# Moving the first use of one weight load later, splitting the last sums, and issuing small transfers from another engine in an attention-plus-MLP gradient kernel

## The chip, the core and the metric

The kernel runs on one core of one Trainium2 chip. The metric is the device time of that core in microseconds (us). Before the change the median of three runs was 423.68 us (423.5 to 424.09).

Engines are named as the profile names them: PE (TensorE: matrix products), PEld (its weight loads), DVE (VectorE), ACT (ScalarE), POOL (GpSimd), SP (SyncE, which here only requests loads). In the traces "SPq" or "ACTq" is the engine's own issuing of a transfer.

## The reference

The forward function is a gate between one decode step of cached attention (32 heads, 4096 keys, head size 128) and a small MLP. The kernel computes its output and all gradients. Cut to what matters:

```python
q = (x @ wq)                                    # 640 -> 32 heads x 128
p = softmax(q . k_cache * Dh**-0.5)             # k_cache, v_cache: 32 x 4096 x 128, bf16
a = (p . v_cache) @ wo
h = x_B @ w1 + b1 ; b = (h * tanh(softplus(h))) @ w2     # w2: 1728 x 640
out = g * a + (1 - g) * b ,  g = sigmoid(sum(x * gate_w))
# returned: out and the gradients of x, k_cache, v_cache, wq, wo, w1, b1, w2, gate_w
```

K and V have to be read once and dK and dV, just as large, have to be written once. Each of the 32 heads has 1 MB of each of the four.

## The kernel before

K and V come in through four buffers each, requested by SP three heads ahead. PE and ACT transpose them, PE forms scores and sums, DVE forms dK and dV as outer products in two halves each, and POOL requests their stores. The MLP runs in the gaps. It is cut into steps that a host-side list hands out, at three "slots" in each head:

```python
def slot(h, p=2, d=1):
    # called three times per head: runs ready steps, at most p of kind "P" (PE)
    # and d of kind "D" (DVE); a step is ready if all steps it names ran in an EARLIER slot
    ...
def load_w2(c):                                  # w2 comes in three pieces, two buffers
    w2cs[c] = mlp.tile([FP, FCC, D], BF16, name="w2c", tag="w2c", bufs=2)
    nc.sync.dma_start(w2cs[c][:], w2_v[:, c * FCC:(c + 1) * FCC, :])
...  # (cut)
for c in range(NCH):                             # NCH = 3 pieces
    add(f"b{c}", "P", b_part(c), ("act2",) + ((f"badd{c - 1}", f"dw2_{c - 1}") if c else ()), H0)
    add(f"badd{c}", "T", b_add, (f"b{c}",), H0)
    for i in range(FCC):
        add(f"dh{c}_{i}", "D", dh_part(c, i), ("act2", f"w2_{c}"), H0)     # DVE reads w2c
    ...  # dw2a, dw2: DVE writes dw2 over w2c, then POOL stores it
    if c < 2: done[f"w2_{c}"] = -1               # the first two pieces are loaded at the start
    else:
        for k in range(4):                       # wait four slots for the buffer's store
            add(f"w2w{k}_{c}", "T", lambda: None, (f"w2w{k - 1}_{c}" if k else f"dw2_{c - 2}",), H0)
        add(f"w2_{c}", "T", lambda c=c: load_w2(c), (f"w2w3_{c}",), H0)    # REQUEST of piece 3
```

The step `w2_2` is done when the load has been *requested*, not when it has landed. The next slot, about 4 us later, may already put the first product with the third piece into DVE's program. DVE runs its program in order, so it waits there.

The start and the end of the kernel also matter here:

```python
nc.sync.dma_start(vec_rows[0:RC, :], x_rows)               # three loads of 1.3 KB, then
nc.sync.dma_start(vec_rows[RC:2 * RC, :], dy_rows)         # the big loads, all on SP
nc.sync.dma_start(vec_rows[2 * RC:3 * RC, :], gw_rows)
load_wq(0); load_wo(0); load_k(0); load_v(0); ...          # (cut)
...
dk_half(H - 1, 0); dk_half(H - 1, 1)
last = [st for st in steps if st[0].startswith("dx")]      # five DVE sums of 1024 columns
...  # the other steps; then the last weight gradient, whose store is the last big one:
nc.gpsimd.dma_start(dwq_v[:, :, CL:], dwq_l[:])
steps.extend(last)                                         # the five sums, 1.22 us each
...  # some 14 small DVE, PE and ACT steps on 128x5 values, then three stores of five rows:
nc.sync.dma_start(out0_rows, fin_rows[0:RC, :])
nc.sync.dma_start(out1_rows, fin_rows[RC:2 * RC, :])
nc.sync.dma_start(out9_rows, fin_rows[2 * RC:3 * RC, :])
```

## Time and profile before

| | before |
|---|---|
| time, median (range) | 423.68 us (423.5 to 424.09) |
| span of the profiled run | 423.3 us |
| moved by DMA | 165.06 MB |
| rate on the plateau | about 422 GB/s |
| 165.06 MB at 422 GB/s | 391.1 us |
| DVE, PE busy | 307.4 us (73%), 306.7 us (72%) |

The page of the kernel before: busy time by engine, then the span in 40 slices of 10.6 us, with busy tenths (9 is 90% or more) and the rate that the DMA engines moved.

```profile
PE 306.7 (72%) x6932; PEld 283.4 (67%) x6932; DVE 307.4 (73%) x794; ACT 174.5 (41%) x394; POOL 50.9 (12%) x92
...
DVE  3359466675699999758306999899999976637981
...
DMA  7999999999999999999983799999999999999991
GB/s 243 424 411 395 422 423 417 424 420 426 422 423 422 423 415 423 422 423 422 414 312 147 292 343 392 412 421 423 420 424 422 424 422 420 424 407 399 411 409 59
DMA packets 26336, 165.06 MB, mean 390 GB/s; under 512 B 2812, under 2 KB 2812, under 8 KB 10012
```

No compute engine is full, and the DMA engines are full nearly everywhere. The rate stands at about 422 GB/s, and three places fall below it: the start (slice 1), a hole (slices 21 to 25) and the end (slice 40). The Trainium skill, "DMA: Bandwidth & Descriptors", section Specifications, gives a fabric ceiling of 435 GB/s; the trace's plateau agrees with it within 3%.

It helps to turn the row of rates into a budget. A slice at rate r loses (422 − r)/422 of its 10.58 us. Summed over all slices that is 32.2 us, and 391.1 + 32.2 is the span of 423.3 us. By part: slices 1 to 4 lose 5.4 us, 21 to 27 lose 15.9 us, and 36 to 40 lose 10.7 us.

The waits of the same kernel: which engine and line waited for what, us in total, times, longest.

```profile
ACT tT L531 <- PE tr L529: 173.1, 138, 21.0
POOL out_dram L568 <- DVE dK_sb L551: 73.6, 10, 23.2
DVE junk L449 <- DMA w2c<-in_B_w_dram: 20.3, 1, 20.3
...
PE qc_ps L258 <- DMA wq_g<-in_A_wq_dram: 3.7, 2, 2.8
...
SPq L781 <- DMA out_dram<-dwq_l: 1.8, 1, 1.8
```

The chain that ended last, in order of time (start, duration, what), around the hole:

```profile
194.50 0.03 SPq L138
...
194.57 30.21 DMA w2c<-in_B_w_dram
...
224.81 0.04 DVE junk L449
```

And the windows of the hole and of the end: stretch in us, its length, busy us of each engine (instructions), granted clock, share of the 16 DMA engines, GB/s.

```profile
200.00:212.00 12.00, 4.80 (x113) 4.34 (x111) 4.52 (x12) 3.38 (x7) 1.06 (x2) 0.83 1.01 411
212.00:224.00 12.00, 0.00 (x0) 0.00 (x0) 0.00 (x0) 0.00 (x0) 0.00 (x0) 0.50 0.82 291
224.00:236.00 12.00, 10.15 (x183) 9.66 (x184) 9.63 (x25) 3.84 (x8) 1.07 (x2) 0.53 0.30 126
...
415.00:419.00 4.00, 0.28 (x1) 0.09 (x1) 0.38 (x2) 0.26 (x1) 0.00 (x0) 0.50 0.06 25
```

The load of the third piece is requested at 194.57 us and lands 30.2 us later, behind the loads already queued. DVE stands still for 20.3 us, and everything behind it in its program stands too: from 212 to 224 us no engine runs a single instruction. While they stand, the queued transfers finish, no new buffer comes free, and DMA falls to 126 GB/s.

The line for 415 to 419 us is worth remembering. A DMA share of 0.06 is one sixteenth, and 25 GB/s is about one sixteenth of 422. For those 4 us one single DMA engine was moving data and the other fifteen had finished.

The start, in the timeline (start, duration, engine, line, what):

```profile
0.74 0.36 SPq L108 DMA_DIRECT2D vec_rows<-in_A_x_dram  x1
...
1.81 0.41 SPq L127 DMA_DIRECT2D wq_g<-in_A_wq_dram  x1
```

The first big load is the fourth that SP issues, 1.07 us after the first.

### The profile page before, as it was taken

To read this page: it belongs to the slowest core of one execution; us is meant where nothing else is said; L and a number is where in the kernel's file an instruction comes from. 1 tells how busy PE (TensorE), PEld (TensorE's weight loads), DVE (VectorE), ACT (ScalarE), POOL (GpSimd) and SP (SyncE) were. 2 spreads that over 40 slices of the span, in tenths; PEclk is the share of its full clock that TensorE was granted. 3 is DMA by queue.
4 is the path that set the end of the run, shared out by engine and by line. 5 is a ranking of instruction groups with operands and counts; after the bars stand their busy time and mean duration, and the time that the engine had idled before them with its cause. 6 is when DMAs were issued, how large, how long until landed. Compare 5 with 4: busy or idle time off the path is not lost.

```text
span 423.3 us, 15629 instructions
## 1 busy us (share of the span) xinstructions
PE 306.7 (72%) x6932; PEld 283.4 (67%) x6932; DVE 307.4 (73%) x794; ACT 174.5 (41%) x394; POOL 50.9 (12%) x92
## 2 busy tenths in 40 slices
PE   2588799988989888488306978887787888838500
PEld 2587798888879777388306877787677787737400
DVE  3359466675699999758306999899999976637981
ACT  2265244444454545144201454645454455515200
POOL 0001111011001111111100111211111121103320
PEclk9999899999998999798855899999999899979855
DMA  7999999999999999999983799999999999999991
GB/s 243 424 411 395 422 423 417 424 420 426 422 423 422 423 415 423 422 423 422 414 312 147 292 343 392 412 421 423 420 424 422 424 422 420 424 407 399 411 409 59
DMA packets 26336, 165.06 MB, mean 390 GB/s; under 512 B 2812, under 2 KB 2812, under 8 KB 10012
## 3 DMA queue, kind: packets, MB, share of 16 engines
q1 hardware_dynamic: 14156, 82.03, 47.6%
q0 software_dynamic: 12112, 82.03, 46.9%
q8 instruction: 54, 0.88, 0.8%
q14 instruction: 14, 0.11, 0.1%
HBM read 82.03 MB, written 82.03 MB: 388 GB/s over the span
## 4 chain that ended last, share of the span: by engine, by line
DVE 32%; DMA 31%; PE 24%; ACT 7%; issue 3%; SPq 1%; ACTq 0%; DVEq 0%
DMA Kn<-in_A_k_cache_dram 13%; PE tr L529 8%; DVE dK_sb L551 8%; DMA w2c<-in_B_w_dram 7%; DVE dV_sb L551 7%; DMA out_dram<-dK_sb 7%; ACT tT L531 6%; DVE junk L354 4%; DMA Vn<-in_A_v_cache_dram 4%; PE sB L648 3%; PE h_ps L383 3%; PE sA L537 3%; PE sA L595 3%; DVE junk L484 2%; DVE junk L268 2%
## 5 line engine op out<-in xcount | busy, mean ns | idle before, releaser
L531 ACT COPY tT<-tr 128x512 f32<-128x512 f32 x256 | 143.1, 588 | 173.4 <-PE tr L529 173.1
L537 PEld LDWEIGHTS <-tT 128*128 128x128 bf16 x2048 | 76.6, 98 | 37.7 <-ACT tT L531 31.6
L529 PE MATMUL tr<-ident_bf,Kn 128*128 128x128 bf16 x1024 | 80.5, 232 | 6.2 <-DMA Kn<-in_A_k_cache_dram 5.1
L551 DVE TENSOR_TENSOR dV_sb<-p_bf,qd 128x2048 bf16<-128x2048 bf16 x64 | 78.0, 1218 | 8.4 <-DMA out_dram<-dK_sb 8.4
L551 DVE TENSOR_TENSOR dK_sb<-ds_bf,qd 128x2048 bf16<-128x2048 bf16 x64 | 77.7, 1215 | 0.0
L529 PE MATMUL tr<-ident_bf,Vn 128*128 128x128 bf16 x1024 | 74.0, 222 | 0.0
L529 PEld LDWEIGHTS <-Kn 128*128 128x128 bf16 x1024 | 67.7, 105 | 7.2 <-DMA Kn<-in_A_k_cache_dram 5.4
L537 PE MATMUL sA<-qdc,tT 128*128 128x48 bf16 x1024 | 49.1, 187 | 23.2 <-ACT dq_all L653 16.4
L529 PEld LDWEIGHTS <-Vn 128*128 128x128 bf16 x1024 | 64.2, 101 | 0.6
L537 PE MATMUL sB<-qdc,tT 128*128 128x48 bf16 x1024 | 46.7, 184 | 0.6 <-ACT tT L531 0.6
L568 POOL DMA_DIRECT2D out_dram<-dK_sb x31 | 19.0, 613 | 169.3 <-DVE rz L617 86.5
L648 PE MATMUL sB<-ds_bf,Kn 128*128 128x48 bf16 x1024 | 32.1, 185 | 9.7 <-DVE ds_bf L637 8.3
L578 POOL DMA_DIRECT2D out_dram<-dV_sb x32 | 18.4, 576 | 164.7 <-DVE dV_sb L551 75.1
L595 PEld LDWEIGHTS <-Vn 128*128 128x128 bf16 x1024 | 30.8, 96 | 10.7 <-issue 10.4
L595 PE MATMUL sA<-e_bf,Vn 128*128 128x48 bf16 x1024 | 31.5, 184 | 7.7 <-DVE zs L615 5.9
L648 PEld LDWEIGHTS <-Kn 128*128 128x128 bf16 x1024 | 29.3, 97 | 10.1 <-issue 10.1
L449 DVE SCALAR_TENSOR_TENSOR junk<-w2c,dm,db_bc 96x640 bf16<-96x640 bf16 x18 | 15.7, 874 | 20.5 <-DMA w2c<-in_B_w_dram 20.3
L599 DVE TENSOR_REDUCE m<-sA 128x1 f32<-128x32 f32 x32 | 6.0, 188 | 32.9 <-PE sA L537 32.7
L268 DVE SCALAR_TENSOR_TENSOR junk<-wo_g,da_bc 128x640 bf16<-128x640 bf16 x32 | 26.2, 820 | 4.3 <-DMA wo_g<-in_A_wo_dram 3.7
L603 PE MATMUL sA<-ident_f,m 128*128 128x128 f32 x32 | 9.6, 301 | 24.8 <-DVE m L599 24.8
L354 DVE SCALAR_TENSOR_TENSOR junk<-wq_g,dq_bc 128x1024 bf16<-128x1024 bf16 x20 | 24.4, 1218 | 0.2
L603 PEld LDWEIGHTS sA<-ident_f,m 128*128 128x128 f32 x32 | 4.5, 140 | 26.4 <-DVE m L599 26.2
(137 smaller groups left out, 293.5 us busy)
## 6 DMA issues: line engine op xcount, KB each, us to landing
Kn<-in_A_k_cache_dram SPq DMA_DIRECT2D x32, 1024.0 KB, 20.4
Vn<-in_A_v_cache_dram SPq DMA_DIRECT2D x32, 1024.0 KB, 27.1
out_dram<-dV_sb POOLq DMA_DIRECT2D x32, 1024.0 KB, 11.1
out_dram<-dK_sb POOLq DMA_DIRECT2D x31, 1024.0 KB, 11.8
wq_g<-in_A_wq_dram SPq DMA_DIRECT2D x4, 1280.0 KB, 20.5
wo_g<-in_A_wo_dram SPq DMA_DIRECT2D x8, 640.0 KB, 17.9
out_dram<-wo_g POOLq DMA_DIRECT2D x8, 640.0 KB, 11.6
out_dram<-dwq_t POOLq DMA_DIRECT2D x5, 896.0 KB, 11.9
```

Of the source, the lines that this page charges most:

```text
L268: nc.vector.scalar_tensor_tensor(junk[:, 0:D], in0=wos[g][:, i, :], scalar=1.0, in1=da_bc[:], op0=ALU.mult, op1=ALU.mult, accum_out=gp["do ...
L354: nc.vector.scalar_tensor_tensor(junk[:], in0=wqs[w][:, rc, :], scalar=1.0, in1=dq_bc[:, w * WG * Dh:(w + 1) * WG * Dh], op0=ALU.mult, op1 ...
L449: nc.vector.scalar_tensor_tensor(junk[0:FP, 0:D], in0=w2cs[c][:, i, :], scalar=m["dm"][:, fc:fc + 1], in1=db_bc[0:FP, :], op0=ALU.mult, op ...
L529: nc.tensor.transpose(tp[:, t, :], src[:, c * 8 + t, :], ident_bf[:])
L531: nc.scalar.copy(f32v(sb[:].rearrange("p a b -> p (a b)")), f32v(tp[:].rearrange("p a b -> p (a b)")))
L537: nc.tensor.matmul(out[:, j:j + W], lhsT=tb[:, t, :], rhs=vec.to_broadcast([P, W]), start=True, stop=True)
L551: nc.vector.tensor_tensor(dst[:, a:b, :].rearrange("p j (a b) -> p j a b", b=2), col[:, a:b, :].unsqueeze(2).to_broadcast([P, n, Dh // 2, 2]),
L568: nc.gpsimd.dma_start(dKv[h], st["dK"][:])
L578: nc.gpsimd.dma_start(dVv[h], st["dV"][:])
L595: nc.tensor.matmul(O, lhsT=vts[h][:, j, :], rhs=st["e"][:, j:j + 1].to_broadcast([P, W]), start=(j == 0), stop=(j == J - 1))
L603: nc.tensor.transpose(MM, m32[:].to_broadcast([P, P]), ident_f[:])
L648: nc.tensor.matmul(DQ, lhsT=kts[h][:, j, :], rhs=ds[:, j, 0:1].to_broadcast([P, W]), start=(j == 0), stop=(j == J - 1))
```

## The change

The change has three parts. The first separates the request of the third `w2` piece from its first use by eight more slots, so that the load lands before DVE gets there. The second halves the last dx sums by head group, so that only half of them remain for the end, and starts the gate's gradient earlier. The third takes the three small vector loads off SP's queue. The result is the same numbers from the same data.

```diff
-    nc.sync.dma_start(vec_rows[0:RC, :], x_rows)          # and the other two
+    nc.scalar.dma_start(vec_rows[0:RC, :], x_rows)
...
-        def dx(rc):
+        def dx(rc, c0, c1, slot_i):                       # sums columns c0:c1 only
...
-        if g % 2 == 1:
-            for rc in range(RC):
-                add(n(f"dx{rc}_"), "D", dx(rc), (n("dqb"),))
+        for rc in range(RC):
+            if g >= NG - 2:                               # last two groups: one half each
+                add(n(f"dx{rc}_"), "D", dx(rc, (g % 2) * GD, (g % 2 + 1) * GD, g - NG + 2 + NW - 1), (n("dqb"),))
+            elif g % 2 == 1:
+                add(n(f"dx{rc}_"), "D", dx(rc, 0, WG * Dh, g // 2), (n("dqb"),))
...
-            add(f"b{c}", "P", b_part(c), ("act2",) + ((f"badd{c - 1}", f"dw2_{c - 1}") if c else ()), H0)
+            add(f"b{c}", "P", b_part(c), ("act2", f"w2_{c}") + ((f"badd{c - 1}",) if c else ()), H0)
...
-                add(f"w2_{c}", "T", lambda c=c: load_w2(c), (f"w2w3_{c}",), H0)
+                add(f"w2l_{c}", "T", lambda c=c: load_w2(c), (f"w2w3_{c}",), H0)
+                for k in range(8):
+                    last = k == 7
+                    add(f"w2_{c}" if last else f"w2x{k}_{c}", "T", lambda: None,
+                        (f"w2x{k - 1}_{c}" if k else f"w2l_{c}",), H0)
...  # dgp, dg_ps, gg moved ahead of the last dx sums (cut)
-    nc.sync.dma_start(out1_rows, fin_rows[RC:2 * RC, :])
+    nc.scalar.dma_start(out1_rows, fin_rows[RC:2 * RC, :])
```

More of the change, by code (lines that the diff above doesn't have):

```diff
@@ L107 @@
     vec_rows = const.tile([3 * RC, P], BF16, name="vec_rows")
-    nc.sync.dma_start(vec_rows[0:RC, :], x_rows)
-    nc.sync.dma_start(vec_rows[RC:2 * RC, :], dy_rows)
-    nc.sync.dma_start(vec_rows[2 * RC:3 * RC, :], gw_rows)
+    nc.scalar.dma_start(vec_rows[0:RC, :], x_rows)
+    nc.scalar.dma_start(vec_rows[RC:2 * RC, :], dy_rows)
+    nc.scalar.dma_start(vec_rows[2 * RC:3 * RC, :], gw_rows)
     kts, vts, wqs, wos = {}, {}, {}, {}
@@ L220 @@
     NW = H // WG
-    dxp = const.tile([P, RC, NW + 2], F32, name="dxp")
+    dxp = const.tile([P, RC, NW + 3], F32, name="dxp")
     dq_bc = const.tile([P, H * Dh], BF16, name="dq_bc")
@@ L349, in dqb @@
             nc.scalar.copy(f32v(dq_bc[:, g * GD:(g + 1) * GD]), f32v(b_ps[:].rearrange("p a b -> p (a b)")))
-        def dx(rc):
+        def dx(rc, c0, c1, slot_i):
             def f():
                 w = g // 2
-                nc.vector.scalar_tensor_tensor(junk[:], in0=wqs[w][:, rc, :], scalar=1.0,
-                                               in1=dq_bc[:, w * WG * Dh:(w + 1) * WG * Dh],
-                                               op0=ALU.mult, op1=ALU.mult, accum_out=dxp[:, rc, w:w + 1])
+                nc.vector.scalar_tensor_tensor(junk[:, c0:c1], in0=wqs[w][:, rc, c0:c1], scalar=1.0,
+                                               in1=dq_bc[:, w * WG * Dh + c0:w * WG * Dh + c1],
+                                               op0=ALU.mult, op1=ALU.mult, accum_out=dxp[:, rc, slot_i:slot_i + 1])
             return f
@@ L485, in f @@
                                                in1=m["dh_bc"][:, a:b], op0=ALU.mult, op1=ALU.mult,
-                                               accum_out=dxp[:, rc, NW + k:NW + k + 1])
+                                               accum_out=dxp[:, rc, NW + 1 + k:NW + 2 + k])
             return f
@@ L717 @@
     nc.gpsimd.dma_start(dwq_v[:, :, CL:], dwq_l[:])
-    steps.extend(last)
-    while steps:
-        slot(H, 9, 9)
     assert len(dwqt) == RC
@@ L725 @@
     fin = C("fin", [P, 3 * RC])
-    ga = C("ga", [P, RC])
-    nc.vector.tensor_scalar(ga[:], a_acc[:], g_all[:], None, ALU.mult)
-    nc.vector.scalar_tensor_tensor(fin[:, 0:RC], in0=b_acc[:], scalar=omg_all[:], in1=ga[:], op0=ALU.mult, op1=ALU.add)
     amb = C("amb", [P, RC])
@@ L736 @@
     nc.tensor.transpose(dg_ps[:], dgp[:].to_broadcast([P, P]), ident_f[:])
+    ga = C("ga", [P, RC])
+    nc.vector.tensor_scalar(ga[:], a_acc[:], g_all[:], None, ALU.mult)
+    nc.vector.scalar_tensor_tensor(fin[:, 0:RC], in0=b_acc[:], scalar=omg_all[:], in1=ga[:], op0=ALU.mult, op1=ALU.add)
+    gg = C("gg", [P, 1])
+    nc.vector.tensor_tensor(gg[:], g_all[:], omg_all[:], ALU.mult)
+    for st in last[:2]:
+        st[2]()
     dg = C("dg", [P, 1])
     nc.vector.reduce_sum(dg[:], dg_ps[:], axis=AX.X)
-    gg = C("gg", [P, 1])
-    nc.vector.tensor_tensor(gg[:], g_all[:], omg_all[:], ALU.mult)
     dz = C("dz", [P, 1])
@@ L743 @@
     nc.vector.tensor_scalar(fin[:, 2 * RC:3 * RC], x_f, dz[:], None, ALU.mult)
+    for st in last[2:]:
+        st[2]()
     dxs = C("dxs", [P, RC])
```

## The prediction

The prediction counts the slices from 0, so its slices 20 to 26 are slices 21 to 27 in the rest of this document.

> **What bounds the kernel now.** The DMA engines. The page gives 165.06 MB; the windows 60-100, 100-140 and 300-340 us run at 422, 422, 423 GB/s. 165.06 MB at 422 is 391 us of the 423.3 us span. The Trainium skill, "DMA: Bandwidth & Descriptors", section Specifications, gives a fabric ceiling of 435 GB/s; the plateau agrees. DVE is next (307 us, 73%). The loss lies in three places of the 40 slices: the start (first slice 243 GB/s, about 4.5 us), one hole in slices 20 to 26 (312, 147, 292, 343, 392, 412, 421: 16 us of plateau), and the end (last slice 59, about 9 us).
>
> **The hole.** In the chain of waits the third w2 load runs from its request at 194.57 to 224.8 us (30.2 us). DVE reaches its first use at 204.6 and idles 20.3 us, its longest wait. DVE works in program order, so the dK and dV products behind it stop; POOL has no store for 23.2 us, ACT waits 21.0 on PE, no K or V buffer comes free, and DMA runs dry.
>
> **What the change does there.** The order of instructions shows the load at the same place on SP; what moves is its use. The first product with the third piece goes from head 15 to head 18, eight slots (three per head), 2.7 heads of 10 to 12 us: about 29 us later. DVE arrived 20 us too early; now it should arrive 5 to 9 us after landing. The load sits behind K and V of head 18 in SP's queue, which head 18 needs just before it, so any wait left should be under 3 us. The 23 MLP pieces behind it (about 20 us of DVE) end near head 27, where DVE has room (41.6 busy of 60 us in 340-400). In 260-340 DVE is 94% busy with DMA still at 419 to 423, so postponed work should not starve DMA; I leave 1 to 2 us of the 16 for that. Gain: about 15 us, all on the path.
>
> **Start.** SP issues three small vector loads (0.74 to 1.77 us) before the first big load at 1.81. On ACT's ring they go in parallel: big loads start about 1.0 us earlier. The same skill page, "Issuing engines are not separate DMA queues", says that issuing elsewhere saves sequencer time only; this is such a case. ACT's table load (1.28 us) ends near 3.1, just when the vectors land. Gain: about 1.0 us.
>
> **End.** Five dx sums of 1024 columns take 1.22 us each after the last stores; halves should take about 0.69 (from 0.82 at 640 and 1.22 at 1024): 2.7 us less, and the dg chain under them saves 0.6. But this chain ends beside another: the last dwq store is requested at 406.8 and lands at 419.1, and SP's end waits 1.8 us on it. That drain is write backlog and does not shrink. I count 0.3 us, not 3.3.
>
> **Sum.** 423.7 - 15.0 - 1.0 - 0.3 = 407.4 us. Range 403.5 to 412. Faster by over 2%: 0.95; within 2%: 0.04; slower: 0.01.
>
> **Right if:** DVE's wait for the w2 load falls from 20.3 to under 3 us; no slice from 4 to 38 is below 390 GB/s; the first big load is issued near 0.75 us; the tail's dx sums take about 0.7 us; the last fin store is issued over 2 us before the last dwq store lands.
>
> **Wrong if:** DVE, with MLP work packed into heads 18 to 27, cannot feed stores at the plateau (slices 23 to 30 below 400); w2 lands over 29 us past the old use; or the drain at the end shortens too (then 404).

## The result, and the profile after

The changed kernel took 417.93 us in the median (417.57 to 418.51, four runs), beside 423.73 us for the kernel before in the same rounds. The ratio is 0.9864 (95% interval 0.9847 to 0.9881), so it is 5.8 us faster where 16.3 us was predicted. Ratios here are the mean time of one kernel's runs over that of the other's runs of the same rounds, so they are not quite the ratio of the medians that are quoted. All runs compared here are fast ones, except that one of the six runs of `e13_ldw` (438.45 us) was slow and is left out of its ratio, and that `e14_tail_ldw` has a single run of unknown state.

The page of the changed kernel (span 415.7 us, slices of 10.4 us):

```profile
DVE  2348666665679999989897688528999997967850
...
DMA  8999999999999999999999999999999999998980
GB/s 280 419 401 335 420 424 417 420 423 423 421 423 420 420 404 415 424 420 423 423 410 426 423 414 411 419 422 381 405 411 423 419 419 422 421 422 351 401 314 14
```

The hole is gone: slices 21 to 26 read 410 to 426 where they read 147 to 412. Yet the last four slices now read 351, 401, 314 and 14 where they read 399, 411, 409 and 59. DVE's first product with the third piece, the last dx sums, and the start (timelines of DVE, SP and ACT of the changed kernel):

```profile
0.74 0.46 SPq L127 DMA_DIRECT2D wq_g<-in_A_wq_dram  x1
...
1.63 0.31 ACTq L110 DMA_DIRECT2D vec_rows<-in_gate_w_dram  x1
...
7.25 0.17 ACT L176 COPY cols_bf<-cols_ps 128x15 bf16<-128x15 bf16 x1 [4.00 <-PE cols_ps L174]
...
234.42 0.87 DVE L451 SCALAR_TENSOR_TENSOR junk<-w2c,dm,db_bc 96x640 bf16<-96x640 bf16 x1
...
396.86 0.69 DVE L354 SCALAR_TENSOR_TENSOR junk<-wq_g,dq_bc 128x512 bf16<-128x512 bf16 x1
...
402.02 1.04 SPq L762 DMA_DIRECT2D out_dram<-fin_rows  x1
```

The product at 234.42 us has no bracket behind it, so it waited for nothing. Every local step came out as intended: no wait for `w2c`, sums of 0.69 us, the first big load at 0.74 us. What was not intended is the ACT copy at 7.25 us. It waited because the vectors now land at about 7.0 us. Before they landed at about 3.0 us, and the same copy ran at 3.23 us.

The waits of the changed kernel that are new or longer:

```profile
PE qc_ps L258 <- DMA wq_g<-in_A_wq_dram: 11.8, 1, 11.8
DVE dj L641 <- PE sB L635: 10.8, 1, 10.8
PE cols_ps L174 <- DMA vec_rows<-in_gate_w_dram: 7.0, 1, 7.0
...
SPq L788 <- DMA out_dram<-dwq_l: 5.4, 1, 5.4
```

PE's longest single wait for a `wq_g` load was 2.8 us before. It is 11.8 us now, ending at 276.6 us. DVE's wait of 10.8 us ends 1.6 us after it, and the slice with 381 GB/s (slice 28, 281 to 291 us) follows directly. SP's wait at the very end for the last big store (`dwq_l`) went from 1.8 us to 5.4 us.

Windows of the changed kernel, in the columns of before:

```profile
212.00:224.00 12.00, 7.91 (x163) 7.36 (x163) 11.32 (x31) 3.90 (x10) 1.18 (x3) 0.75 1.01 415
...
376.00:380.00 4.00, 2.53 (x62) 2.40 (x62) 3.55 (x9) 0.65 (x2) 1.66 (x3) 0.80 0.63 262
...
402.00:404.00 2.00, 0.00 (x0) 0.00 (x0) 0.00 (x0) 0.00 (x0) 0.00 (x0) 0.50 0.61 223
404.00:411.00 7.00, 0.00 (x0) 0.00 (x0) 0.00 (x0) 0.00 (x0) 0.00 (x0) 0.50 0.06 25
```

From 404 to 411 us all work is done, and 25 GB/s at a share of 0.06 means that fifteen DMA engines have finished and one still moves its share. That stretch was 4 us long before (415 to 419) and is 7 us long now. It grew although nothing in the change touches those stores.

The trace shows the same thing from another side. A big transfer here adds 16 to its semaphore, one for each part. The Trainium skill, "DMA: Bandwidth & Descriptors", section "Why a DMA increments its semaphore by 16 and not by 1", says why: "a DMA runs on up to 16 SDMA engines that finish independently, and the semaphore counts them." The trace records each increment, so one can read how much later the sixteenth part came than the fifteenth. I call this the lag.

```
kernel    transfer landing at                lag of the 16th part behind the 15th, us
before    loads at 205 to 211 us             5.5 to 6.6
before    w2 piece 3 at 224.8 us             4.2
before    first load after the hole, 243 us  0.7
before    loads at 246 to 377 us             0.7 to 3.6
before    last big store                     3.5
after     a load at 195 us                   5.3
after     a load at 235 us                   7.7
after     wq_g at 276.5 us                   7.1
after     loads at 323 to 364 us             12.0 to 13.5
after     last big store                     7.2
```

So the last part of each load falls behind the other fifteen. In the kernel before, the hole let it catch up, from 6.6 us to 0.7 us, and the lag of the loads stayed under 4 us from there on. (Loads have to be compared with loads: a store at 214 us, before the hole, lagged by 0.4 us only.) In the kernel after there is no such hole, and the lag of the loads grows to 13.5 us. It does not grow steadily: in both kernels it stays under 3 us until about 158 us, though the queues are full long before that. The trace does not say which engine carried a part. That it is one and the same engine throughout is inferred from the stretch at one sixteenth at the end.

This lag lies under waits that were seen above. Fifteen parts of the `wq_g` load had landed by 269.4 us; the sixteenth came at 276.5 us, and there PE's wait of 11.8 us ended. The dip at 376 to 380 us follows a wait of DVE (4.1 us) for a dK store to leave its buffer: fifteen parts were done by 367.2 us, the sixteenth at 375.0 us.

The budget of plateau time, worked out from the slices as before, for both kernels and for the `w2` part alone (the run `e1_w2_only` below):

| lost, in us at 422 GB/s | before | after | w2 part alone |
|---|---|---|---|
| start, slices 1 to 4 | 5.4 | 6.2 | 5.2 |
| slices 5 to 20 | 0.3 | 0.8 | 0.4 |
| hole, slices 21 to 27 | 15.9 | 0.7 | 1.3 |
| slices 28 to 35 | −0.1 | 1.8 | 2.0 |
| end, slices 36 to 40 | 10.7 | 15.0 | 15.0 |
| sum, plus 391.1 = span | 32.2 | 24.6 | 23.9 |

About 15 us of hole were filled, as predicted. About 4.3 us of them came back at the end and about 2 in slices 28 to 35. The table divides the span; by itself it does not say why a part grew.

### The profile page after: what moved, and what is told of

Read it like the earlier page. It is cut to its first block, busy times and chain, and to the rows that moved or that the text cites. A ratio compares the mean times of both kernels' runs of the same rounds, so it can differ in the third digit from the quotient of the medians.

```text
span 415.7 us, 15639 instructions
## 1 busy us (share of the span) xinstructions
PE 305.6 (74%) x6932; PEld 281.1 (68%) x6932; DVE 308.2 (74%) x804; ACT 174.4 (42%) x394; POOL 49.3 (12%) x92
## 4 chain that ended last, share of the span: by engine, by line
DMA 37%; DVE 30%; PE 21%; ACT 6%; issue 2%; ACTq 0%; DVEq 0%
DMA Kn<-in_A_k_cache_dram 30%; PE tr L535 7%; DVE dK_sb L557 7%; DVE dV_sb L557 6%; DMA out_dram<-dK_sb 6%; ACT tT L537 5%; DVE junk L354 4%; PE sA L601 3%; PE sA L543 3%; PE sB L654 3%; DVE junk L268 3%; PE h_ps L385 2%; DVE junk L486 2%; DMA vec_rows<-in_gate_w_dram 1%; DVE wo_g L343 1%
## 5 line engine op out<-in xcount | busy, mean ns | idle before, releaser
L535 PE MATMUL tr<-ident_bf,Kn 128*128 128x128 bf16 x1024 | 79.2, 230 | 9.4 <-DMA Kn<-in_A_k_cache_dram 8.2
L535 PEld LDWEIGHTS <-Kn 128*128 128x128 bf16 x1024 | 66.2, 104 | 10.9 <-DMA Kn<-in_A_k_cache_dram 9.3
L535 PE MATMUL tr<-ident_bf,Vn 128*128 128x128 bf16 x1024 | 72.8, 221 | 0.2 <-DMA Vn<-in_A_v_cache_dram 0.2
L543 PE MATMUL sA<-qdc,tT 128*128 128x48 bf16 x1024 | 49.2, 188 | 23.0 <-ACT dq_all L659 16.3
L535 PEld LDWEIGHTS <-Vn 128*128 128x128 bf16 x1024 | 63.2, 100 | 1.4 <-issue 0.7
L601 PEld LDWEIGHTS <-Vn 128*128 128x128 bf16 x1024 | 30.3, 96 | 10.4 <-issue 10.3
L574 POOL DMA_DIRECT2D out_dram<-dK_sb x31 | 17.7, 570 | 153.1 <-DVE rz L623 84.6
L654 PEld LDWEIGHTS <-Kn 128*128 128x128 bf16 x1024 | 29.7, 97 | 8.3 <-issue 8.3
L354 DVE SCALAR_TENSOR_TENSOR junk<-wq_g,dq_bc 128x1024 bf16<-128x1024 bf16 (+1 forms) x25 | 25.1, 1004 | 0.2
L385 PE MATMUL h_ps<-cols_bf,w_sb 128*96 128x1 bf16 x90 | 18.3, 314 | 1.2 <-ACT qd L279 0.5
L641 DVE TENSOR_SCALAR_CACHE_REDUCE dj<-sB,rz 128x128 f32<-128x128 f32 x32 | 11.1, 345 | 10.8 <-PE sB L635 10.8
L385 PEld LDWEIGHTS <-w_sb 128*96 128x96 bf16 x90 | 17.6, 272 | 1.6 <-issue 0.6
```

The source lines that it names most:

```text
L354: nc.vector.scalar_tensor_tensor(junk[:, c0:c1], in0=wqs[w][:, rc, c0:c1], scalar=1.0, in1=dq_bc[:, w * WG * Dh + c0:w * WG * Dh + c1], op ...
L385: nc.tensor.matmul(hps[a][:, fc:fc + 1], lhsT=w1_sb[:, rc, :].rearrange("p (q c) -> p q c", c=FCN)[:, :, fc], rhs=x_bf[:, rc:rc + 1], star ...
L535: nc.tensor.transpose(tp[:, t, :], src[:, c * 8 + t, :], ident_bf[:])
L543: nc.tensor.matmul(out[:, j:j + W], lhsT=tb[:, t, :], rhs=vec.to_broadcast([P, W]), start=True, stop=True)
L574: nc.gpsimd.dma_start(dKv[h], st["dK"][:])
L601: nc.tensor.matmul(O, lhsT=vts[h][:, j, :], rhs=st["e"][:, j:j + 1].to_broadcast([P, W]), start=(j == 0), stop=(j == J - 1))
```

## The experiments

My theory after reading the traces: the hole is filled, but a hole does not cost its full size, because a trailing DMA engine catches up in it; without it that engine sets when the late loads and the last store land. The rivals: the two small parts of the change cost what is missing; or DVE, with the MLP packed later, no longer feeds stores; or the trailing is made by PE's instruction fetches, or by PE itself. In the table "lag" is that of the last big store, and the ratio is to the kernel before in the same rounds.

| run | time, us | ratio (95%) | lag, us |
|---|---|---|---|
| e1_w2_only | 416.32 | 0.9808 (0.9794–0.9821) | 7.2 |
| e2_tail_only | 425.12 | 1.0013 (1.0–1.0025) | 2.5 |
| e3_vec_only | 424.77 | 1.0006 (0.9992–1.002) | 2.4 |
| e4_after_sp_vec | 417.34 | 0.9835 (0.9821–0.9849) | 7.25 |
| e5_half_dq | 413.36 | 0.9757 (0.9741–0.9772) | 6.0 |
| e6_half_dq_o | 412.61 | 0.9729 (0.9714–0.9744) | 5.7 |
| e7_slots4 | 415.48 | 0.9804 (0.979–0.9818) | 6.5 |
| e8_slots2 | 420.3 | 0.99 (0.9876–0.9924) | 3.5 |
| e9_one_col | 423.29 | 0.9962 (0.9929–0.9994) | 6.5 |
| e10_wide | 446.1 | 1.0529 (1.0498–1.056) | 0.02 |
| e11_wide_dq | 417.07 | 0.9841 (0.9815–0.9867) | 5.5 |
| e12_half_ldw | 422.85 | 0.9963 (0.994–0.9986) | 4.2 |
| e13_ldw | 430.49 | 1.014 (1.011–1.0171) | 1.2 |
| e14_tail_ldw (one look) | 452.56 | none | 8.3 |
| e15_after | 417.7 | 0.9844 (0.9824–0.9864) | 7.3 |
| e16_w2_vec | 417.23 | 0.9836 (0.9814–0.9859) | 6.5 |
| e17_slots4 | 415.84 | 0.9805 (0.9785–0.9824) | 6.4 |

The kernel before had medians of 423.94 to 424.46 us in these rounds. Runs 1 to 4 shared one chip, as did 5 to 8, 9 to 13, and 15 to 17. A lag comes from the one profiled run of each kernel. It is 3.5, 2.5 and 2.4 us in the three kernels that keep the hole (before, e2, e3), and 7.2 and 6.5 us in e1 and e16, so differences of about 1 us in it say little.

### The three parts, each alone

Run `e1_w2_only` is the kernel before with only the two hunks of `mlp_steps` that move the `w2` use.

```diff
+            add(f"b{c}", "P", b_part(c), ("act2", f"w2_{c}") + ((f"badd{c - 1}",) if c else ()), H0)
+                add(f"w2l_{c}", ...); for k in range(8): add(... eight empty steps ...)
```

> Only the later use of the third w2 piece. The prediction on record would give 408.7 us (15 us less). Theory A (the filled hole is partly paid back at the end, where one of the sixteen DMA engines trails the others by 7 us instead of 3.5): about 412 to 416, DVE's wait for w2 gone, all DMA slices from 5 to 37 near 420, and a last-of-sixteen landing of the last store 6 to 8 us after the fifteenth. Theory B (the longer end comes from the reordered tail, which delays the last dwq store): 409 to 411 and a trailing engine of about 3.5 us.

It took 416.32 us, 8.1 us less than the median of before (424.46) in those rounds, and was faster than the whole change. That is just above the range of theory A and far from the 408.7 us of the prediction. The slices were not all near 420, as theory A had expected: slices 28 and 37 read 371 and 357. Its row of rates:

```profile
GB/s 242 423 418 393 421 425 412 422 424 421 423 424 422 420 411 418 426 420 420 426 416 423 421 414 411 418 400 371 406 418 426 416 421 415 421 421 357 385 322 15
```

and its window near the end:

```profile
404.00:411.00 7.00, 0.28 (x1) 0.09 (x1) 0.18 (x1) 0.25 (x1) 0.00 (x0) 0.50 0.06 24
```

The hole is filled and the same 7 us of a single engine stand at the end, without the other two parts of the change. So what is missing is mainly in the effect of the `w2` part itself. This is the term that the prediction put at 15 us.

Run `e2_tail_only` is the kernel before with the split dx sums, the reordered small steps and `out1` on ACT.

```diff
+            if g >= NG - 2: add(... dx of one half ...)
+    for st in last[:2]: st[2]()        # two sums, then dg, then the other three
+    nc.scalar.dma_start(out1_rows, ...)
```

> Only the split dx sums and the reordered small outputs. Theory A: 422.7 to 424, as the end is set by the write drain and not by DVE. Theory B: slower by 1 to 3 us, since POOL issues the last dwq store about 1.5 us later after DVE has made it. If DVE set the end, as the change intends: 420.5.

It took 425.12 us, ratio 1.0013: no gain, and the interval ends just at 1.0. DVE still waited 21.9 us for `w2c`, as it should. The tail's shorter work gains nothing; in the profile before it was not that work that ended last, as SP waited 1.8 us more for the last `dwq` store.

Run `e3_vec_only` only moves the three vector loads.

```diff
-    nc.sync.dma_start(vec_rows[...], ...)
+    nc.scalar.dma_start(vec_rows[...], ...)
```

> Only the vector loads on ACT's ring. The prediction on record: 1.0 us faster (422.7). Theory A (the small loads now land behind packets of the big ones, near 7 us instead of 3, so head 0 starts later and K buffers come free later while the loads ran ahead): 0 to 2 us slower, vectors landing after 6 us, and a deeper DMA dip near 30 to 36 us.

It took 424.77 us, ratio 1.0006: the same. PE waited until 6.9 us for the vectors, so the late landing belongs to this part of the change. The big loads start 1.07 us earlier, and no gain shows.

Run `e4_after_sp_vec` is the changed kernel with those loads back on SP.

```diff
-    nc.scalar.dma_start(vec_rows[...], ...)
+    nc.sync.dma_start(vec_rows[...], ...)
```

> The changed kernel with the vector loads back on SP's ring. Theory A: 416 to 417.5 (0.5 to 2 us faster than the changed kernel's 417.9); the prediction on record would have it 1.0 us slower (418.9).

It took 417.34 us, ratio 0.9835. Against `e1_w2_only` on the same chip that is 1.0 us slower, and the only difference is the tail part. On this chip the tail part therefore costs about 1 us when the hole is filled: all four of its runs are slower than all four of e1. Why was not found. The same comparison on another chip, `e15_after` against `e16_w2_vec` below, shows 0.5 us, with runs that overlap.

### How large must the hole be before it costs anything?

Runs `e7_slots4` and `e8_slots2` are `e1_w2_only` with four and with two empty slots in place of eight. They open part of the hole again.

```diff
-                for k in range(8):
+                for k in range(4):      # e8: range(2)
```

> e1 with the third w2 piece used four slots later than it was in the kernel before, not eight. DVE then waits about 6 us for it (20.3 less four slots of 3.6), and DMA has a hole of some 3 to 5 us. Theory A (the trailing engine works on through the hole and sets the end): within 1.0 us of e1, 415.5 to 417.5. If a DMA hole costs what it lacks in bytes: 419 to 421.

> e1 with two slots. DVE waits about 13 us and DMA has a hole of some 8 to 10 us. Theory A: the first 4 us or so are free, so 418 to 421. If a hole costs what it lacks: 423 to 426, that is no gain or nearly none over before, which has a hole of 16 us.

With four slots the time was 415.48 us, as good as eight. PE waited 5.6 us for the load in the profiled run, and slices 22 to 26 lost 1.2 us of plateau, which cost nothing that could be measured. With two slots the median was 420.3 us, with runs in two clusters (417.39 and 418.75, and four from 420.12 to 420.96); why it is spread is open. The profiled run is the fastest of them, 417.39 us. Its wait and its rates:

```profile
PE bp L438 <- DMA w2c<-in_B_w_dram: 20.0, 1, 20.0
```

```profile
GB/s 242 422 419 400 423 425 412 424 423 423 420 424 422 424 407 418 424 422 423 421 420 293 303 334 400 424 422 422 421 423 423 424 422 425 420 423 424 417 388 42
```

This pair has no other difference in the code. In `e8_slots2` slices 21 to 27 lose 8.8 us of plateau, and in `e1_w2_only` 1.3 us: 7.5 us more hole. Yet the spans of the two profiled runs are 415.6 and 415.1 us. The rest came back: slices 28 to 35 lose nothing (2.0 in e1), and slices 36 to 40 lose 10.2 us (15.0 in e1), with a lag of 3.5 us instead of 7.2. So a hole in the middle of a full queue is partly, in that run almost wholly, paid for by a shorter end. But the profiled run of e8 is the fastest of its six, and that of e1 is the slowest of its four (416.83 us), and they ran on two chips. Over all six runs the median is 4 us over that of e1, about half of 7.5; since only the fastest run has a trace, the two numbers do not belong to the same run. In the trace of e8 the loads that land from 266 to 369 us lag by 1.4 us at most, though the rate is on the plateau. So full queues alone do not make the lag grow.

### What makes one engine trail: fewer PE instructions

The page lists 54 packets of instructions (0.88 MB) in the kernel before and in the changed one. The Trainium skill, "Runtime: NRT & Kernel Launch", section "Instruction fetch mechanics", says that an engine's instructions are refilled in blocks of 16 KiB, fetched by its sequencer through a DMA queue of its own, and that this is "mostly hidden". In the trace such a packet took about 1 us. Fetches that all sat on one DMA engine would make that engine trail. Runs `e5_half_dq` and `e6_half_dq_o` are `e1_w2_only` with fewer PE instructions. They give wrong results: they sum only every second key block, with twice the columns so that PE's work stays alike.

```diff
-        for j in range(J):
-            nc.tensor.matmul(DQ, lhsT=kts[h][:, j, :], rhs=ds[:, j, 0:1].to_broadcast([P, W]), ...)
+        for j in range(0, J, 2):
+            nc.tensor.matmul(B[:, 128:128 + 2 * W], lhsT=kts[h][:, j, :], rhs=ds[:, j, 0:1].to_broadcast([P, 2 * W]), ...)
         # e6: the same for o_part as well
```

> Base is e1 (only w2 moved; 416.3 us). Wrong results on purpose: the dQ product runs over every second j with twice the columns, so PE has 1024 fewer instructions (of 13864) at the same columns in all; all other traffic is the same. Theory R (one DMA engine trails because it also fetches PE's instructions, 54 packets of 16 KB with about 1 us each): 50 such packets, the trailing engine ends 1 to 4 us less late (7.2 before), time 1 to 4 us less: 412.5 to 415.5. Theory N (the trailing has another cause): 416.3 within 0.5, trailing 7 us.

> As e5, with the o product also over every second j: 2048 fewer PE instructions, 46 instruction packets. Theory R: twice e5's gain, 2 to 8 us, so 408 to 414.5, trailing 0 to 5 us. Theory N: 416.3 within 0.7, trailing 7 us.

They took 413.36 and 412.61 us: ratios 0.9757 and 0.9729 where e1 has 0.9808, so about 2.2 and 3.3 us less. Against `e7_slots4` on the same chip (415.48 us) it is 2.1 and 2.9 us. The lag was 6.0 and 5.7 us, where e1 has 7.2 but e7 has 6.5, so in the lag no clear effect shows. The times lie in theory R's ranges, but e6 gained less than twice as much as e5, and its lag is over the 5 us that the theory allowed. For e6 the rates and the queue of instructions:

```profile
GB/s 245 424 419 392 424 423 416 425 425 425 421 424 423 424 423 418 425 422 423 424 409 420 424 423 420 419 427 395 408 411 426 423 416 427 419 424 388 418 341 14
...
q8 instruction: 46, 0.75, 0.7%
```

The end lost 12.7 us of plateau instead of 15.0. These two kernels are faster, but two things fell at once: fetches and PE's own work. The next runs tried to separate them.

### Controls that failed

Run `e9_one_col` is e1 with all instructions kept, but with one column instead of 48 in those products: less PE work, the same fetches.

```diff
-                nc.tensor.matmul(O, ..., rhs=st["e"][:, j:j + 1].to_broadcast([P, W]), ...)
+                nc.tensor.matmul(O[:, 0:1], ..., rhs=st["e"][:, j:j + 1], ...)      # and DQ[:, 0:1]
```

> Control for e5 and e6, base e1, right results: the o and dQ products take one column instead of 48, so PE does less work in 2048 of its matmuls, but has the same 13864 instructions and 54 instruction packets. Theory R (instruction traffic): as e1, 416.3 within 0.8, trailing engine near 7 us. If e5 and e6 were faster because PE had less to do: 412.5 to 414.5.

The result is correct, and the time was 423.29 us instead of less than e1. The page suggests why, with the granted clock in tenths:

```profile
PEclk9998665767879988696989969958959698998655
...
GB/s 243 422 415 409 424 423 418 421 424 385 380 330 302 358 369 396 422 425 420 418 422 402 423 422 417 420 426 423 422 422 425 407 394 424 425 420 393 417 341 14
```

The mean granted clock fell from 0.918 (e1) to 0.822, PE took 36% of the chain that ended last instead of 21%, so PE came onto the path, and slices 10 to 16 fell as low as 302 GB/s. The Trainium skill, "TensorE: Matmul & The Clock Gate", says in Part 1 that activity releases the throttle; this run agrees. So the 48 columns, of which one is used, kept the clock up in this kernel. As a control the run says nothing about fetches.

Run `e10_wide` keeps the result correct with 1984 fewer PE instructions: two score columns as weights against 256 columns of K or V, and a small product that picks the right halves. Run `e11_wide_dq` does so for dQ only.

```diff
+        for j in range(0, J, 2):
+            nc.tensor.matmul(B[0:2, 256:512], lhsT=ds[:, j:j + 2, 0],
+                             rhs=kts[h][:, j:j + 2, :].rearrange("p a b -> p (a b)"), ...)
+        nc.scalar.copy(q2, B[0:2, 256:512]);  pick(DQ[:, 0:1], q2)      # e10: for O too
```

> Right results with 1984 fewer PE instructions than e1: o and dQ each as 16 products with two columns as weights and 256 columns moving, the two right blocks picked out by two small products after a copy on ACT. Theory R: instruction packets from 54 to 46, so like e6, 412 to 414, if PE's longer products (256 columns, about 0.8 us more per product chain and head, estimated from the 128-column matmuls' share in the trace) do not put PE on the path; if they do, 415 to 422, with DMA slices under 410 in many places.

> As e10, for dQ alone: 992 fewer PE instructions, 50 packets. Theory R: like e5, 413.5 to 415.5; PE on the path: 415 to 419.

The wide form of both took 446.1 us:

```profile
PE 404.1 (90%) x6164; PEld 341.4 (76%) x6164; DVE 309.7 (69%) x794; ACT 199.3 (45%) x458; POOL 50.3 (11%) x92
```

PE became the limit (71% of the chain that ended last), and with unsaturated queues the lag was 0.02 us. The wide dQ alone took 417.07 us with a lag of 5.5 us: shorter than e1's, but PE was busy for 84% of the span, which may have taken the gain back (not shown). It is not a better kernel.

Runs `e12_half_ldw` and `e13_ldw` add 2048 weight loads of one column that nothing uses: to e6, to bring its fetches back to 54 packets, and to e1.

```diff
+        for _ in range(32):
+            nc.tensor.ldweights(ident_bf[:, 0:1])        # twice in each head
```

> e6 (2048 fewer PE instructions, 412.6 us) with 2048 weight loads of one column, whose weights no product uses, so the instruction count is e1's again (54 packets) while the products stay halved. Wrong results on purpose, as e6. Theory R (instruction traffic): back to e1's 415.5 to 417. If the lighter PE made e6 fast: 412 to 413.5.

> e1 (416.3 us) with the same 2048 unused weight loads: right results, 62 instruction packets. Theory R: 2 to 5 us slower, 418.5 to 421, trailing engine later than 7 us. Otherwise: 416.3 within 0.8, unless PE comes onto the path, which would show as DMA slices under 410 in the middle.

They took 422.85 and 430.49 us, that is 10 and 14 us more than e6 and e1 (which ran on other chips). That is far more than the theory of fetches asked for, and its cause lies elsewhere: in e12 slices 12 to 16 fell to 330 to 384 GB/s, and in e13 slices 9 to 16 were not full either. The added loads put PE onto the path: PE and its weight loads take 38% and 45% of the chain that ended last, where e1 has 21%. Like e9 these runs do not separate fetches from PE's work. Their lags of 4.2 and 1.2 us go with queues that were not full; e9, whose queues were not full either, has 6.5 us.

### A direct look at a fetch

Run `e14_tail_ldw` is e1 with 1536 unused weight loads after PE's last transpose, so that instruction fetches fall into the stretch in which only the trailing engine moves data. If fetches went through that engine, its own transfers would pause.

```diff
+    for _ in range(1536):
+        nc.tensor.ldweights(ident_bf[:, 0:1])            # after the transpose of the last outputs
```

> e1 with 1536 unused weight loads of one column on PE after its last transpose, so that about six 16 KB instruction packets are fetched while only the trailing engine still moves data. Theory R: the packets stand in that engine's row (it moves no data meanwhile), and its last store lands 1 us later per packet: it trails by 9 to 13 us. Theory N: they run beside it, its row has no holes, and it trails by 7 us. The time itself is longer in both, as PE has to run the loads (about 22 us).

A 16 KB packet of instructions that took 1.2 us fell into that stretch. The windows of e14 (DMA share and GB/s are the last two columns):

```profile
404.00:405.00 1.00, 0.00 (x0) 1.00 (x83) 0.00 (x0) 0.04 (x1) 0.00 (x0) 0.50 0.06 20
405.00:406.00 1.00, 0.00 (x0) 1.00 (x36) 0.00 (x0) 0.00 (x0) 0.00 (x0) 0.50 0.07 23
406.00:407.00 1.00, 0.00 (x0) 1.00 (x36) 0.00 (x0) 0.00 (x0) 0.00 (x0) 0.50 0.14 41
407.00:408.00 1.00, 0.00 (x0) 1.00 (x36) 0.00 (x0) 0.00 (x0) 0.00 (x0) 0.50 0.06 24
```

In the us of the fetch the share doubled to 0.14 and the rate rose from 23 to 41 GB/s: a second engine carried the fetch beside the trailing one. The trailing engine's 4 KB packets went on without a break, and the four that began during the fetch took 179, 178, 173 and 173 ns. So this fetch did not pass through the trailing engine, and the theory of fetches in that engine's row falls for the one fetch that could be looked at. The same packets say something else: 4 KB took 179 ns in the median here and 159 ns in e1, where PE was idle (165 ns in the kernel before), and 5 KB took 219 instead of 196 ns. The trailing engine was about 12% slower than in e1 while PE ran weight loads. The lag was 8.3 us, between what the two theories had expected. This is one profiled run with a time of 452.56 us; what it has over e1 comes from the added loads, which took 44.4 us, twice what was expected.

### Does it repeat, and which version is best?

The last three runs are on a chip of their own: the changed kernel again, e1 with the vector loads on ACT, and e7 again.

```diff
 # e15: the changed kernel, no edit
 # e16: e1 with
+    nc.scalar.dma_start(vec_rows[...], ...)
 # e17: e7, no edit
```

> The changed kernel again, on the chip of the next two. Ratio to before as in its first measurement, 0.985 to 0.988.

> e1 with the vector loads on ACT's ring (so the changed kernel without the split sums and reordered outputs). If the vectors cost 1.2 us and the tail 1.1 us as the first batch says: ratio 0.982 to 0.985, between e1 (0.981) and the changed kernel (0.986). If the vector loads are free: as e1, 0.981.

> The four-slot kernel again: 0.979 to 0.982, so 2 to 3 us faster than the changed kernel on the same chip.

The changed kernel took 417.7 us (0.9844, just below the expected 0.985), e16 417.23 us (0.9836) and e17 415.84 us (0.9805). The result of the change repeats: 6.6 us by this ratio, 5.8 by the first. The `w2` part with four slots and nothing else is faster than the changed kernel by 1.9 us on the same chip, and its interval (0.9785 to 0.9824) just touches that of the changed kernel (0.9824 to 0.9864). It beats both kernels, by about 8.3 us the first. The vector part on top of `w2` seems to cost about 1 us: 0.9836 in e16 and 0.9808 in e1. But e1 ran on another chip, and the intervals overlap a little, so this is not shown.

## Why the prediction was wrong

The direction was right and the size was not: 407.4 us was predicted (403.5 to 412), 417.93 us was measured. The step that failed is "Gain: about 15 us, all on the path", point 2 below.

1. **What bounds the kernel, and the mechanism of the hole: right.** The wait for `w2c` went from 20.3 us to none, DVE reached the product with it at 204.6 us before and at 234.4 us after (29.8 us later, where about 29 was predicted; 4.7 us after the landing, where 5 to 9 was predicted), and slices 21 to 26 are full.

2. **"Gain: about 15 us, all on the path": wrong, and the main error.** The term measured 8.1 us, with `e1_w2_only`. About 15 us of hole were filled, but 4.3 us came back at the end and about 2 us in slices 28 to 35, where a `wq_g` load arrived late enough for PE to wait 11.8 us. What failed is the assumption that plateau time lost in a hole is lost for good. In the kernel before, the trailing engine recovered in the hole (lag of the loads from 6.6 to 0.7 us); without the hole its lag is 12 to 13.5 us on late loads and about 7 us on the last store. The late `wq_g` load and the last store landed late by just these sixteenth parts. Before and e1, alike but for the `w2` use, show the size: 14.6 us of hole less, 8.2 us of span less in the profiled runs. e1 and e8 show it from the other side (7.5 us of hole more, 0.5 us of span more in the two profiled runs, about 4 us in the medians). That the trailing engine is the reason is read from the landings; no run changed its lag and nothing else.

3. **"Postponed work should not starve DMA": right.** The sign against it, a slice of 23 to 30 below 400, did appear once (381 in slice 28). The waits put it on the late `wq_g` load and on DVE waiting for PE behind it, not on DVE being too busy. The sign "no slice from 4 to 38 below 390" failed too; in the numbers of this document (one higher) it failed in slices 28 (381), 37 (351) and 39 (314).

4. **"Start … Gain: about 1.0 us": wrong.** The big load was issued at 0.74 us as said. The step that failed is that ACT's table load would end "just when the vectors land": they landed at about 7.0 us, behind the big loads, and not at 3.0. The skill's section "Issuing engines are not separate DMA queues" was quoted for the gain: it says that issuing elsewhere saves sequencer time only. The saved time showed no gain here: the small loads, which stood first in line before, now landed 4 us later. Measured: no change alone (e3), and perhaps about 1 us lost on top of the `w2` part (e16 against e1, two chips, overlapping intervals). Slices 3 and 4 fell from 411 and 395 to 401 and 335.

5. **"End … I count 0.3 us": right that it is little, but no gain shows.** The sums took 0.69 us and the last small stores were issued at 402.0 us, 9 us before the last big store had landed, as predicted. So it was right that the shorter chain would hardly count. Measured: nothing alone (e2), 1.0 us lost on top of the `w2` part on one chip (e4 against e1) and 0.5 us on another (e15 against e16, within the scatter).

6. **"That drain is write backlog and does not shrink": wrong as a reading.** Of the drain before, 415 to 419 us was one engine at 25 GB/s, not a backlog on sixteen. It could have been read from the window of before, by its DMA share of 0.06. It did not shrink; it grew from 4 to 7 us, and SP's wait for the last store from 1.8 to 5.4 us. Read in this way, it would have shown that the engines do not keep step, which raises the question of what a hole in the middle does to the end.

With measured terms the sum closes: −8.1 us (e1), about +1 us (tail, e4 against e1) and up to +1 us (vectors, e16 against e1) give −6 to −7 us, where −5.8 and −6.6 us were measured in the two sets of runs.

What stays open: why one engine trails, and why its lag grows in some stretches and not in others. Kernels with fewer PE instructions are faster (e5, e6), but their lag is hardly shorter than that of e7 on the same chip. The trailing engine's packets were 12% slower than in e1 while PE ran weight loads (e14, one run). Fetches did not pass through it in the one case that could be seen. A rival that no run tests is the queue of the stores: POOL issues all the big ones, and no run moved them. The controls that should have separated fetches from PE's own work brought PE onto the path (e9, e12, e13). Also open are the tail part's 1 us and the two clusters of e8.

## What to carry to other kernels

Before you count a hole in a saturated DMA queue as pure gain, look at the last microseconds: a DMA share of one sixteenth there says that one engine runs behind the other fifteen, and part of what you fill in the middle may come back at the end, as it did here. Put only as much distance between a load and its use as the load needs (four slots were as good as eight here), and test each part of a change alone, since two of the three parts here, each with a plausible local reason, gained nothing and may have cost up to a microsecond each. Small loads that something waits for landed sooner ahead of the big ones in the same queue (3.0 us) than from a queue beside them (7.0 us).

## What the Trainium skill lacked or had wrong

- "DMA: Bandwidth & Descriptors" says that the engines of one transfer finish independently, but not how far apart they can get. Its section "Latency and other measured facts" calls two of the sixteen engines usually slower in traces, without a size; the traces here do not name the engine, so no run shows whether it is one of these. Under full queues the runs show the last part 12.0 to 13.5 us behind the fifteenth on late loads and about 7 us on the last store, and that a gap in the queue lets it catch up (loads from 6.6 to 0.7 us).
- The same page, section "Issuing engines are not separate DMA queues", says that issuing from another engine only saves sequencer time. It does not say what it may cost: three small loads issued from ACT beside the big ones on SP landed at about 7.0 us instead of 3.0 us.
- "Runtime: NRT & Kernel Launch", section "Instruction fetch mechanics", calls the fetch "mostly hidden" and gives no duration. The packets of 16 KB took about 1 us each here, 1.2 us in e14, on a DMA engine that data transfers use too. No run here shows what they cost.
- No page was found that says that PE's work slows a DMA engine. In e14, one run, the 4 KB packets of the one engine still moving took 179 ns while PE ran weight loads, and 159 ns in e1 with PE idle.
- "TensorE: Matmul & The Clock Gate" agrees on the throttle. The number to add is that products of one column instead of 48 took the mean granted clock from 0.918 to 0.822 and the time from 416.32 to 423.29 us (on two chips).
